# Blocks of 512 tokens, weight conversion on VectorE, and one pass over d_ff per block

## The chip, the cores and the metric

The kernel runs on one core of one Trainium2 chip. The metric is the device time of one execution in microseconds. Engines are named as the profile names them: PE (TensorE; PEld is its weight load), DVE (VectorE), ACT (ScalarE), POOL (GpSimd), SP (which issues all DMAs).

## What is computed

Three layers follow each other: linear attention with decay (retention), a feed-forward layer, and a second feed-forward layer with a softmax gate and a norm. Inputs are float32 for q, k, v; the weights are float64 in the kernel's input.

```python
# retention: B, H, S, D = 4, 8, 768, 64
gamma = 1 - 2.0 ** (-5 - arange(H))
for t in range(S):
    state = gamma * state + outer(k[t], v[t])
    y[t] = q[t] @ state / sqrt(D)
# layer 1: x is 3072 x 512, w_in 512 x 2048, w_out 2048 x 512
h = x @ w_in
g = where(h >= 1, h, where(h <= -1, 0, (h + 1) ** 2 / 4))
x2 = g @ w_out
# layer 2: w_in 512 x 1024, w_out 1024 x 512
h = x2 @ w_in
e = exp(h - max(h)); u = h * e / (sum(e) + 1e-9)
out = ((u - mean(u)) / sqrt(var(u) + 1e-6) * g_ln) @ w_out
```

## The kernel before

**Products.** Every large product is done with operands split into a high and a low part (`split`, L117: ACT copies the high part with rounding, DVE subtracts it for the low one), as high x high + low x high + high x low.

**Phase A** is layer 1, over blocks of BLK = 384 tokens (8 blocks) and 16 parts of d_ff of 128 each. A slot is one block with one part f. `moe_h` (L318) makes the first product of a slot, 12 matmuls into one PSUM bank hp, and then the activation: DVE clamps hp, ACT takes a Relu of hp and a square, DVE adds, and the split follows. `moe_out` (L346) makes the second product, 12 matmuls that add to four banks acc, two slots later (GB = 3). At a block's end the four banks are copied to xs and stored to DRAM (x2d).

**Order of the slots** (`segs`, L275): block 0 over parts 0 to 5, block 1 over parts 0 to 11, block 0 over the rest, block 1 over the rest, then blocks 2 to 7 each over all 16. Between its two stretches the sum of a block is put aside in DRAM (x2p) and added later. So new weights are taken up at about half the rate in the first 32 slots.

**Weights.** Each part f has a tile of w_in and one of w_out, 512 KB each as float64 words. `conv_w` (L133) turns one into a high and a low float32r part: ACT takes the absolute value of the high word, DVE clamps it (L140) and shifts it (L143), ACT turns the low word into a float (L142), DVE merges sign and bits (L144), POOL adds low and high words as integers (L145), ACT copies the high part (L149), and POOL, or for 14 tiles DVE, subtracts it (L150). `weights_slot` (L302) loads a tile LD = 6 or 7 slots ahead of its first use and converts it CL = 3 or 2 slots ahead. Raw tiles, converted tiles and the q, k, v of the first NF32 units share one pool of 33 tiles (tag w, L98). In the last block `w2_conv` converts the 16 tiles of layer 2, two a slot from f = 2 on.

**Attention** goes over 24 units of 128 tokens with all heads (`attention`, L157), three units to a block. The first NF32 = 6 units use float32 products, the others split operands (kh, qs). Scores get a 0/1 causal mask (DVE for the first six, a POOL selection for the others). Decay is applied to v (vdec), to the result pv (xtab, two DVE products per unit), and to the state (gdec, on POOL). The units' steps are put into slots a few slots ahead of their block (`sched`, L285).

**Phase B** is layer 2, in 24 tiles of 128 tokens: `h2` (L456), `trans` (L498), `outp` (L509).

**What sets the order.** The program is written once, in this order of slots; a planner then gives each engine its fixed list. The order of issue is the order of priority; a free engine may be given ready work of lower priority, and a tile is given out when the pool has one free. SP issues its DMAs strictly in its list's order.

Of the kernel before, what the change touches and what calls it, by code (L numbers as in the profile page):

```python
# [26 lines left out]
BLK = 384  # L27
# [6 lines left out]
# words of the high half of a float64, read as float32: 2^-127 and the largest float32r  # L34
LO_I = (0,1)
LO_O = range(4,16)
LO_2 = 0
V_POOL = 3
DMA_ORDER = -99
PSV = 0  # L40
HPW = 0
HPL = 8
SA = 6
SB = 12
LD = 6
CL = 3
HPC = 0
PHB = 3
XL_POOL = 0
QL_POOL = 0  # L50
NF32 = 6
WM_BUFS = 3
WP_BUFS = 3
QK_BUFS = 3
QS_BUFS = 1
KV_BUFS = 1
QN_BUFS = 1
GATE = 6
SM_BUFS = 3
STEP0 = 7  # L60
W0 = -4
WARM = 40
C_ACT = 0
SHIFT = 0
X2 = 22
PER = 5
HP_ATT = 1000
HP_FROM = 6
# [5 lines left out]
def kernel(  # L74
# [16 lines left out]
    order = ExitStack()  # L91
    if DMA_ORDER > -99:
        order.enter_context(tc.manual_schedule(engines={mybir.EngineType.SP}))
# [4 lines left out]
    wp = ctx.enter_context(tc.tile_pool(name="wp", bufs=33))  # L98
# [8 lines left out]
    neg1 = const.tile([128, 1], F32, tag="neg1", name="neg1")  # L107
    mask = const.tile([128, 1, C], F32, tag="mask", name="mask")
# [5 lines left out]
    def fl(t):  # L114
        return t.bitcast(F32)

    def split(src, hi, lo, hi_eng=None, lo_eng=None):  # L117
        if hi_eng is ve:
            ve.tensor_copy(hi, src)
        else:  # L120
            sc.activation(hi, src, AF.Copy)  # L121
        (lo_eng or ve).tensor_tensor(out=lo, in0=src, in1=fl(hi), op=ALU.subtract)  # L122

# [9 lines left out]
    def conv_w(raw, scale=None, lo_eng=None):  # L133
        lw, hw = raw[:, :, 0], raw[:, :, 1]
        m = cv.tile([128, 512], F32, tag="wm", name="wm", bufs=WM_BUFS)
        p = cv.tile([128, 512], F32, tag="wp", name="wp", bufs=WP_BUFS)
# [17 lines left out]
    # Heads go in pairs (even, odd); the even one takes partitions 0-63 of queries, keys and  # L154
    # state, the odd one 64-127, and TensorE works on both halves of its array at a time.
    # In x the halves of pairs 2 and 3 are swapped, and so are the rows of w_in.
    def attention(u, env):  # L157
# [6 lines left out]
        kv = (wp if exact else attp).tile([128, 2, H, D], F32, tag="w" if exact else "kv", name="kv", bufs=None if exact else KV_BUFS)  # L164
        with (ExitStack() if u < GATE else tc.issue_after(state["last_w"].ins)):
            if exact:
                qk = wp.tile([128, 2, NPAIR, C], F32, tag="w", name="qk")
                nc.sync.dma_start(qk, qk_t[b, c])
                qks = [qk, qk]
                qn = qk[:, 0]  # L170
            else:
                qks = []
                for o in range(2):
                    qk = attp.tile([128, 2, NPAIR, C], F32, tag="qk", name="qk", bufs=QK_BUFS)
                    for dup in range(2):
                        nc.sync.dma_start(qk[64 * dup:64 * dup + 64], qk_t[b, c, 64 * o:64 * o + 64])
                    qks.append(qk)
                if not first:
                    qn = attp.tile([128, NPAIR, C], F32, tag="qn", name="qn", bufs=QN_BUFS)
# [4 lines left out]
        sm = []  # L184
        if exact:
            yield
            qp = [ppool.tile([128, NPAIR, C], F32, tag=ptag, name=f"qp{o}") for o in range(2)]
            for p in range(NPAIR):
                for o in range(2):
                    r = slice(64 * o, 64 * o + 64)  # L190
                    pe.matmul(qp[o][:, p, :], qk[r, 1, p, :], qk[r, 0, p, :], start=True, stop=True)
        for o in range(2):
            if not exact:
                raw = qks[o]
                kh = cv.tile([128, NPAIR, C], F32R, tag="wm", name="kh", bufs=WM_BUFS)
                qs = attp.tile([128, NPAIR, 2, C], F32R, tag="qs", name="qs", bufs=QS_BUFS)
# [3 lines left out]
                (gp if QL_POOL else ve).tensor_tensor(out=qs[:, :, 1, :], in0=raw[:, 0], in1=fl(qs[:, :, 0, :]), op=ALU.subtract)  # L200
                yield
                t = attp.tile([128, NPAIR, C], F32, tag="sm", name="sm", bufs=SM_BUFS)
# [8 lines left out]
                gp.affine_select(out=t, in_=t, pattern=[[0, NPAIR], [1, C]], compare_op=ALU.is_ge,  # L211
                                 fill=0.0, base=0, channel_multiplier=-1)
            else:
                t = attp.tile([128, NPAIR, C], F32, tag="sm", name="sm", bufs=SM_BUFS)
# [383 lines left out]
```

## Time and profile before

| | us |
|---|---|
| median of 3 runs | 972.96 (972.27 to 973.82) |
| span of the profiled execution (first to last instruction) | 969.7 |
| its own time | not listed beside the span |
| PE busy | 936.3 (97%) |
| DVE busy | 741.9 (77%) |
| ACT busy | 455.6 (47%) |
| POOL busy | 201.0 (21%) |
| DMA | 87.03 MB, mean 90 GB/s |

Shares are means over stages with different limits, so they are to be read by stretch. A row of the profile names line, engine, operation, output and input tiles; in a group's row the mean is of one instruction's span, and spans of neighbours on one engine can overlap. Matmuls are pipelined: their mean span is longer than the time from one to the next.

### The profile page before, as it was taken

What the parts mean: (1) busy time and instruction counts of PE and PEld (TensorE: products, weight loads), DVE (VectorE), ACT (ScalarE), POOL (GpSimd) and SP (SyncE); (2) the same over time, 40 slices, a digit from 0 to 9 for tenths busy, and PEclk for the clock granted to TensorE, in tenths of its full rate; (3) what the DMA queues carried; (4) which work ended last, traced back from release to release, by engine and by line L of the source; (5) the groups of instructions that cost most, each with busy time, mean ns of one, the idle gap of its engine ahead of it and who ended that gap; (6) DMA issues with size and microseconds to landing.
All of it is one profiled execution on the core that took longest, in us unless ns stands there. A gap on an engine that the chain in (4) does not pass through costs nothing.

```text
span 969.7 us, 14961 instructions
## 1 busy us (share of the span) xinstructions
PE 936.3 (97%) x5560; PEld 856.5 (88%) x5560; DVE 741.9 (77%) x1593; ACT 455.6 (47%) x905; POOL 201.0 (21%) x177
## 2 busy tenths in 40 slices
PE   8798898999999999999999999989999999999998
PEld 7588888999999999999999999969888888888886
DVE  6999999877666666655664574997788888888885
ACT  3557676545545545544553464664433333333322
POOL 2754544212211221111220120662000000000000
PEclk9899999999999999999999999999999999999999
DMA  9902823154233232420320230311111011010000
GB/s 366 360 1 82 250 82 114 48 169 126 79 98 116 92 97 80 128 77 22 114 72 12 107 143 1 122 64 69 66 55 42 35 55 54 23 61 28 22 23 33
DMA packets 31465, 87.03 MB, mean 90 GB/s; under 512 B 4384, under 2 KB 10656, under 8 KB 31392
## 3 DMA queue, kind: packets, MB, share of 16 engines
q1 hardware_dynamic: 31392, 86.08, 26.9%
q8 instruction: 44, 0.72, 0.3%
q14 instruction: 29, 0.24, 0.1%
HBM read 71.90 MB, written 14.16 MB: 89 GB/s over the span
## 4 chain that ended last, share of the span: by engine, by line
PE 74%; DVE 18%; issue 3%; ACT 2%; DMA 2%; SPq 0%; POOL 0%; ACTq 0%; DVEq 0%; POOLq 0%
PE acc L360 19%; PE hp L325 19%; PE h2p L464 14%; PE op L516 14%; DVE wm L144 3%; DVE cs L340 3%; DVE wm L140 2%; PE pv L233 2%; PE tp L505 2%; DVE gl L122 2%; PE qp L206 2%; DVE wm L143 2%; DVE cs L337 2%; PE pv L229 2%; DVE w L150 1%
## 5 line engine op out<-in xcount | busy, mean ns | idle before, releaser
L360 PE MATMUL acc<-gh,w 128*128 128x384 f32 x1024 | 214.3, 339 | 9.6 <-ACT gh L121 7.6
L325 PE MATMUL hp<-xh,w 128*128 128x384 f32 x1024 | 209.6, 340 | 5.6 <-ACT rr L338 3.9
L360 PEld LDWEIGHTS acc<-gh,w 128*128 128x128 f32 x1024 | 180.1, 189 | 15.4 <-ACT gh L121 10.4
L325 PEld LDWEIGHTS hp<-xh,w 128*128 128x128 f32 x1024 | 179.0, 189 | 12.2 <-ACT rr L338 6.2
L338 ACT ACTIVATE rr<-hp,neg 128x384 f32<-128x384 f32 x128 | 74.1, 579 | 161.4 <-DVE cs L337 161.2
L340 DVE TENSOR_TENSOR cs<-cs,rr 128x384 f32<-128x384 f32 x128 | 86.0, 672 | 77.7 <-ACT cs L339 76.8
L360 PE MATMUL acc<-gl,w 128*128 128x384 f32 x512 | 121.7, 338 | 4.8 <-DVE gl L122 4.8
L325 PE MATMUL hp<-xl,w 128*128 128x384 f32 x512 | 111.8, 338 | 0.0
L122 DVE TENSOR_TENSOR gl<-cs,gh 128x384 fp32r<-128x384 f32 x128 | 85.5, 668 | 26.7 <-ACT gh L121 24.5
L121 ACT ACTIVATE gh<-cs 128x384 fp32r<-128x384 f32 x128 | 66.8, 522 | 65.7 <-DVE cs L340 65.5
L464 PE MATMUL h2p<-w,x2h 128*128 128x512 f32 x384 | 97.4, 395 | 0.0
L360 PEld LDWEIGHTS acc<-gl,w 128*128 128x128 f32 x512 | 90.3, 188 | 8.1 <-DVE gl L122 7.5
L337 DVE TENSOR_SCALAR cs<-hp 128x384 f32<-128x384 f32 x128 | 70.5, 551 | 32.3 <-PE hp L325 31.8
L325 PEld LDWEIGHTS hp<-xl,w 128*128 128x128 f32 x512 | 91.7, 190 | 0.5 <-DVE xl L122 0.3
L516 PE MATMUL op<-w,lh 128*128 128x512 f32 x384 | 91.4, 390 | 0.2 <-ACT lh L121 0.2
L145 POOL TENSOR_TENSOR wm<-wm,wp 128x512 int32<-128x512 int32 x48 | 69.1, 1440 | 88.0 <-DVE wm L144 70.6
L516 PEld LDWEIGHTS op<-w,lh 128*128 128x128 f32 x384 | 71.9, 188 | 15.4 <-ACT lh L121 0.5
L464 PEld LDWEIGHTS h2p<-w,x2h 128*128 128x128 f32 x384 | 70.5, 188 | 13.5
L339 ACT ACTIVATE cs<-cs,half 128x384 f32<-128x384 f32 x128 | 77.6, 606 | 2.5 <-DVE cs L337 2.5
L150 POOL TENSOR_TENSOR w<-wm,w 128x512 fp32r<-128x512 f32 x34 | 49.6, 1461 | 52.2 <-ACT w L149 51.9
L211 POOL TENSOR_SCALAR_AFFINE_SELECT sm<-sm 128x512 f32<-128x512 f32 x36 | 36.3, 1010 | 99.6 <-DVE sm L210 99.6
L254 POOL TENSOR_TENSOR state<-state,gdec 64x256 f32<-64x256 f32 x32 | 22.0, 688 | 165.1 <-DVE state L253 163.9
(79 smaller groups left out, 1299.7 us busy)
## 6 DMA issues: line engine op xcount, KB each, us to landing
qk<-in_qk_t_dram SPq DMA_DIRECT2D x72, 256.0 KB, 3.8
kv<-in_kv_t_dram SPq DMA_DIRECT2D x24, 512.0 KB, 3.8
w_raw<-in_w_in_dram SPq DMA_DIRECT2D x24, 512.0 KB, 7.3
w_raw<-in_w_out_dram SPq DMA_DIRECT2D x24, 512.0 KB, 6.7
x2d<-xs SPq DMA_DIRECT2D x32, 192.0 KB, 2.0
x2r<-x2d SPq DMA_DIRECT2D x8, 768.0 KB, 4.3
out_dram<-o SPq DMA_DIRECT2D x24, 256.0 KB, 2.0
qn<-in_qk_t_dram SPq DMA_DIRECT2D x15, 256.0 KB, 3.1
```

The costliest lines, as they stand in the source:

```text
L121: sc.activation(hi, src, AF.Copy)
L122: (lo_eng or ve).tensor_tensor(out=lo, in0=src, in1=fl(hi), op=ALU.subtract)
L145: gp.tensor_tensor(out=mi, in0=mi, in1=p.bitcast(I32), op=ALU.add)
L150: (lo_eng or gp).tensor_tensor(out=w[:, 1, :], in0=m, in1=fl(w[:, 0, :]), op=ALU.subtract)
L325: pe.matmul(hp, l[:, k * 128:(k + 1) * 128], r[:, k, :], start=(n == 0), stop=(n == 3 * KD - 1))
L337: ve.tensor_scalar(cs, hp, -1.0, 1.0, op0=ALU.max, op1=ALU.min)
L338: sc.activation(rr, hp, AF.Relu, bias=neg1)
L339: sc.activation(cs, cs, AF.Square, bias=half, scale=0.5)
L340: ve.tensor_tensor(out=cs, in0=cs, in1=rr, op=ALU.add)
L360: pe.matmul(acc[d][:, :BLK], l[:, d * 128:(d + 1) * 128], r, start=(first and m == 1), stop=(last and m == 3))
L464: pe.matmul(hps[n], l[:, k, :], w2i[k, n][part], start=(m == 0), stop=(m == 3 * KD - 1))
L516: pe.matmul(op, l[:, f, :], w2o[f][part], start=(n == 0), stop=(n == 3 * NF2 - 1))
```

## The change

Five things change together.
- BLK is 512: 6 blocks, 4 units of attention to a block, 96 slots, matmuls of 512 columns in phase A.
- Each block goes over all 16 parts at once; no sum is put aside. All 32 weight tiles have their first use in block 0's 16 slots, with loads 7 or 8 and conversions 4 or 3 slots ahead.
- `conv_w` does the integer add and the low part on DVE; a scale is folded into the last two instructions. In the last block, 2 and 1 tiles of layer 2 are converted in turn.
- The activation is max(h, square of the clamped half): the Relu and the add go, DVE takes the maximum of hp in PSUM and the square.
- Decay goes into tables: scores are multiplied by one table dmat that holds mask and decay, q is scaled by qdec (DVE in the first 8 units, POOL in the others), k by vdec on POOL, the state by ACT. xt and the POOL selections go, pv takes one bank, and 8 units instead of 6 are done in float32.

```diff
-BLK = 384
+BLK = 512
-LD = 6
-CL = 3
-NF32 = 6
-GATE = 6
+LD, CL = 7, 4
+NF32 = 2 * CPB
+GATE = 2 * CPB
...
-    def conv_w(raw, scale=None, lo_eng=None):
+    def conv_w(raw, scale=None):
...
-        gp.tensor_tensor(out=mi, in0=mi, in1=p.bitcast(I32), op=ALU.add)
-        if scale is not None:
-            ve.tensor_scalar(m, m, scale, None, op0=ALU.mult)
+        ve.tensor_tensor(out=mi, in0=mi, in1=p.bitcast(I32), op=ALU.add)
         w = wp.tile([128, 2, 512], F32R, tag="w", name="w")
-        sc.activation(w[:, 0, :], m, AF.Copy)
-        (lo_eng or gp).tensor_tensor(out=w[:, 1, :], in0=m, in1=fl(w[:, 0, :]), op=ALU.subtract)
-        return w[:, 0, :], w[:, 1, :]
+        hi, lo = w[:, 0, :], w[:, 1, :]
+        if scale is None:
+            sc.activation(hi, m, AF.Copy)
+            ve.tensor_tensor(out=lo, in0=m, in1=fl(hi), op=ALU.subtract)
+        else:
+            sc.activation(hi, m, AF.Copy, scale=scale)
+            ve.scalar_tensor_tensor(lo, m, scale, fl(hi), op0=ALU.mult, op1=ALU.subtract)
+        return hi, lo
...
-        (gp if u >= V_POOL else ve).tensor_tensor(out=kv[:, 1], in0=kv[:, 1], in1=vdec.to_broadcast([128, H, D]), op=ALU.mult)
...
+            if not first:
+                qn = attp.tile([128, NPAIR, C], F32, tag="qn", name="qn", bufs=1)
+                ve.tensor_tensor(out=qn, in0=qk[:, 0], in1=qdec, op=ALU.mult)
+        elif not first:
+            gp.tensor_tensor(out=qn, in0=qn, in1=qdec, op=ALU.mult)
+        if not last:
+            gp.tensor_tensor(out=kv[:, 0], in0=kv[:, 0], in1=vdec.to_broadcast([128, H, D]), op=ALU.mult)
...
+            if exact:
+                ve.tensor_tensor(out=t, in0=qp[o], in1=dmat[:, o], op=ALU.mult)
...
-                gp.affine_select(out=t, in_=t, pattern=[[0, NPAIR], [1, C]], compare_op=ALU.is_ge,
-                                 fill=0.0, base=0, channel_multiplier=-1)
+                ve.tensor_tensor(out=t, in0=t, in1=dmat[:, o], op=ALU.mult)
...
-        for g in range(2):
-            d = slice(2 * g, 2 * g + 2)
-            ve.tensor_tensor(out=xt[:, d], in0=pv[g], in1=xtab[:, d], op=ALU.mult)
-        split(xt, xh[:, :, tk], xl[:, :, tk], lo_eng=gp if XL_POOL else None)
+        split(pv, xh[:, :, tk], xl[:, :, tk])
...
+        if not first:
+            for p in range(NPAIR):
+                sc.activation(st[:, p, :], st[:, p, :], AF.Copy, scale=gdec[:, p, :])
...
+    def tables():
+        nc.sync.dma_start(vdec, vdec_d)
+        for o in range(2):
+            for dup in range(2):
+                nc.sync.dma_start(dmat[64 * dup:64 * dup + 64, o], xtab_d[64 * o:64 * o + 64])
+        nc.sync.dma_start(gdec, gdec_d)
+        nc.sync.dma_start(qdec, xtab_d)
+        for o in range(2):
+            ve.tensor_tensor(out=dmat[:, o], in0=dmat[:, o], in1=vdec[:, o::2].to_broadcast([128, NPAIR, C]), op=ALU.mult)
+            gp.affine_select(out=dmat[:, o], in_=dmat[:, o], pattern=[[0, NPAIR], [1, C]], compare_op=ALU.is_ge,
+                             fill=0.0, base=0, channel_multiplier=-1)
+        gp.tensor_tensor(out=qdec, in0=qdec, in1=gdec.to_broadcast([128, NPAIR, C]), op=ALU.mult)
...
-    segs = [(0, 0, SA), (1, 0, SB), (0, SA, NF), (1, SB, NF)] + [(b, 0, NF) for b in range(2, NBLK)]
+    segs = [(b, 0, NF) for b in range(NBLK)]
...
-        x = (k - 3, SA - 3 + k, X2 + 3 * k)[blk] if blk < 3 else base[blk] - NF + PER * k + SHIFT
+        x = k - CPB if blk == 0 else base[blk] - NF + PER * k + 2
...
-            at = max(first_use[f], W0 + 2 * f)
+            at = first_use[f]
...
-            ve.tensor_scalar(cs, hp, -1.0, 1.0, op0=ALU.max, op1=ALU.min)
-            sc.activation(rr, hp, AF.Relu, bias=neg1)
-            sc.activation(cs, cs, AF.Square, bias=half, scale=0.5)
-        ve.tensor_tensor(out=cs, in0=cs, in1=rr, op=ALU.add)
+        ve.tensor_scalar(cs, hp, -1.0, 1.0, op0=ALU.max, op1=ALU.min)
+        sc.activation(cs, cs, AF.Square, bias=half, scale=0.5)
+        ve.tensor_tensor(out=cs, in0=hp, in1=cs, op=ALU.max)
...
-            if f >= 2:
-                w2_conv(2)
-                w2_step(2)
+            if 2 <= f < 13:
+                w2_conv(2 - f % 2)
+                w2_step(2 - f % 2)
```

## Rows read from the trace of the kernel before

**Rows 1.** Busy time by stretch: us; PE, PEld, DVE, ACT, POOL; PEclk, DMA share, GB/s.
```profile
0.00:180.00 180.00, 157.69 (x1028) 141.84 (x1029) 167.93 (x258) 107.82 (x201) 88.53 (x73) 0.96 0.49 171
180.00:600.00 420.00, 419.50 (x2778) 407.80 (x2777) 269.53 (x494) 208.93 (x424) 73.25 (x77) 1.00 0.30 91
600.00:685.40 85.40, 78.76 (x427) 73.43 (x427) 70.04 (x100) 49.81 (x92) 39.22 (x27) 1.00 0.21 72
685.40:969.70 284.30, 280.32 (x1332) 233.46 (x1330) 234.38 (x742) 88.99 (x191) 0.00 (x0) 1.00 0.12 42
```

**Rows 2.** Chain of waits in order of time: start us, us, what.
```profile
522.08 2.08 PE hp L325 x12
...
524.16 2.08 PE acc L360 x12
...
718.38 5.48 PE h2p L464 x24
723.86 5.44 PE op L516 x24
```

**Rows 3.** Busy time by stretch, matmuls of line L325 alone.
```profile
0.00:180.00 180.00, 66.27 (x316) 0.96 0.49 171
180.00:600.00 420.00, 198.25 (x1030) 1.00 0.30 91
600.00:685.40 85.40, 36.57 (x192) 1.00 0.21 72
```

**Rows 4.** Busy time by stretch, matmuls of line L360 alone.
```profile
0.00:180.00 180.00, 59.85 (x288) 0.96 0.49 171
180.00:600.00 420.00, 200.19 (x1028) 1.00 0.30 91
600.00:685.40 85.40, 43.36 (x221) 1.00 0.21 72
```

**Rows 5.** Busy time by stretch, matmuls of line L233 (tile pv) alone.
```profile
180.00:600.00 420.00, 20.50 (x256) 1.00 0.30 91
```

**Rows 6.** Instructions of one line: min/median/max ns, first and last start us.
```profile
L140 DVE TENSOR_SCALAR wm<-wm x48: 410/420/1522, 15.4 to 657.1; 128x512 f32<-128x512 f32 x48
L143 DVE TENSOR_SCALAR wm<-wm x48: 409/417/1511, 16.1 to 659.0; 128x512 uint32<-128x512 uint32 x48
L144 DVE SCALAR_TENSOR_TENSOR wm<-w_raw,wm x48: 672/681/1776, 17.4 to 659.8; 128x512 uint32<-128x512 uint32 x48
L145 POOL TENSOR_TENSOR wm<-wm,wp x48: 1264/1404/2067, 18.3 to 660.6; 128x512 int32<-128x512 int32 x48
```

**Rows 7.** Groups of DVE, 0 to 180 us: count | busy us, mean ns | idle before.
```profile
L144 DVE SCALAR_TENSOR_TENSOR wm<-w_raw,wm 128x512 uint32<-128x512 uint32 x32 | 27.0, 846 | 0.2
L143 DVE TENSOR_SCALAR wm<-wm 128x512 uint32<-128x512 uint32 x32 | 21.9, 687 | 0.2
L140 DVE TENSOR_SCALAR wm<-wm 128x512 f32<-128x512 f32 x32 | 20.3, 640 | 0.1
L150 DVE TENSOR_TENSOR w<-wm,w 128x512 fp32r<-128x512 f32 x14 | 15.8, 1129 | 0.0
L215 DVE TENSOR_TENSOR sm<-qp,mask 128x512 f32<-128x512 f32 x12 | 8.0, 682 | 0.4 <-PE qp L191 0.4
```

**Rows 8.** Timeline of DVE, 174 to 182 us: start us, us, instruction.
```profile
175.03 0.68 DVE L144 SCALAR_TENSOR_TENSOR wm<-w_raw,wm 128x512 uint32<-128x512 uint32 x1
175.63 0.68 DVE L150 TENSOR_TENSOR w<-wm,w 128x512 fp32r<-128x512 f32 x1
...
179.72 0.69 DVE L150 TENSOR_TENSOR w<-wm,w 128x512 fp32r<-128x512 f32 x1
```

**Rows 9.** Groups of DVE over the whole span: count | busy us, mean ns.
```profile
L476 DVE TENSOR_TENSOR u<-h2p,e 128x512 f32<-128x512 f32 x48 | 32.7, 690 | 8.3 <-ACT e L474 8.2
L253 DVE TENSOR_TENSOR state<-sp,state 64x256 f32<-64x256 f32 x32 | 13.5, 421 | 6.9 <-PE sp L245 6.1
```

**Rows 10.** Waits of the DMA queue: us in total, times, longest us.
```profile
SPq L130 <- DVE wm L144: 91.3, 18, 38.1
```

More of the change, by code (lines that the diff above doesn't have):

```diff
@@ L115, in fl, with split @@
         return t.bitcast(F32)
[L117 to L122, printed above, removed]
+    def split(src, hi, lo):
+        sc.activation(hi, src, AF.Copy)
+        ve.tensor_tensor(out=lo, in0=src, in1=fl(hi), op=ALU.subtract)
     wi, wo = {}, {}
@@ L199, in attention @@
                 ve.tensor_tensor(out=kh[64:128], in0=raw[64:128, 1], in1=fl(kh[64:128]), op=ALU.subtract)
-                (gp if QL_POOL else ve).tensor_tensor(out=qs[:, :, 1, :], in0=raw[:, 0], in1=fl(qs[:, :, 0, :]), op=ALU.subtract)
+                ve.tensor_tensor(out=qs[:, :, 1, :], in0=raw[:, 0], in1=fl(qs[:, :, 0, :]), op=ALU.subtract)
                 yield
-                t = attp.tile([128, NPAIR, C], F32, tag="sm", name="sm", bufs=SM_BUFS)
                 for g in range(2):
@@ L224, in attention @@
         tk = slice(cb * C, cb * C + C)
-        pv = [ppool.tile([128, 2, C], F32, tag=ptag, name=f"pv{g}") for g in range(2)]
+        pv = ppool.tile([128, NPAIR, C], F32, tag=ptag, name="pv")
         if not first:
             for p in range(NPAIR):
-                pe.matmul(pv[p // 2][:, p % 2, :], st[:, p, :], qn[:, p, :],
-                          start=(p % 2 == 0), stop=False, skip_group_check=True)
+                pe.matmul(pv[:, p, :], st[:, p, :], qn[:, p, :],
+                          start=(p == 0), stop=False, skip_group_check=True)
@@ L231, in attention @@
         for p in range(NPAIR):
             for o in range(2):
-                pe.matmul(pv[p // 2][64 * o:64 * o + 64, p % 2, :], kv[:, 1, 2 * p + o, :], sm[o][:, p, :],
-                          start=(first and p % 2 == 0), stop=(p % 2 == 1), skip_group_check=True)
-        xt = attp.tile([128, NPAIR, C], F32, tag="xt", name="xt", bufs=1)
-        for g in range(2):
-            d = slice(2 * g, 2 * g + 2)
-            ve.tensor_tensor(out=xt[:, d], in0=pv[g], in1=xtab[:, d], op=ALU.mult)
@@ L239, in attention @@
-        split(xt, xh[:, :, tk], xl[:, :, tk], lo_eng=gp if XL_POOL else None)
+                pe.matmul(pv[64 * o:64 * o + 64, p, :], kv[:, 1, 2 * p + o, :], sm[o][:, p, :],
+                          start=(first and p == 0), stop=(p == NPAIR - 1), skip_group_check=True)
+        if not last:
+            sp = ppool.tile([128, NPAIR, D], F32, tag=ptag, name="sp")
+            for p in range(NPAIR):
+                for o in range(2):
+                    pe.matmul(sp[64 * o:64 * o + 64, p, :], kv[:, 0, 2 * p + o, :], kv[:, 1, 2 * p + o, :],
+                              start=True, stop=True)
@@ L240, in attention @@
+        split(pv, xh[:, :, tk], xl[:, :, tk])
         if last:
             return
-        sp = ppool.tile([128, NPAIR, D], F32, tag=ptag, name="sp")
-        for p in range(NPAIR):
-            for o in range(2):
-                pe.matmul(sp[64 * o:64 * o + 64, p, :], kv[:, 0, 2 * p + o, :], kv[:, 1, 2 * p + o, :],
-                          start=True, stop=True)
+        if not first:
+            for p in range(NPAIR):
+                sc.activation(st[:, p, :], st[:, p, :], AF.Copy, scale=gdec[:, p, :])
@@ L247, in attention @@
         for o in range(2):
             r = slice(64 * o, 64 * o + 64)
-            d, g = st[r, :, r], gdec[r].to_broadcast([64, NPAIR, D])
             if first:
-                ve.tensor_tensor(out=d, in0=sp[r], in1=g, op=ALU.mult)
+                ve.tensor_copy(st[r, :, r], sp[r])
             else:
-                ve.tensor_tensor(out=d, in0=sp[r], in1=d, op=ALU.add)
-                gp.tensor_tensor(out=d, in0=d, in1=g, op=ALU.mult)
+                ve.tensor_tensor(out=st[r, :, r], in0=sp[r], in1=st[r, :, r], op=ALU.add)
@@ L296, in att_slot @@
                 gens[u] = attention(u, env)
-            with (tc.high_priority(offset=HP_ATT) if HP_ATT and u >= HP_FROM else ExitStack()):
+            with (tc.high_priority(offset=HP_ATT) if u >= NF32 else ExitStack()):
                 next(gens[u], None)
@@ L363, in moe_out @@
             for d in range(KD):
-                xs = moe.tile([128, BLK], F32, tag="xs", name="xs")
+                xs = moe.tile([128, BLK], F32, tag="cs", name="xs", bufs=3)
                 a = acc[d][:, :BLK]
@@ L385 @@
         if s == min(sched):
-            for t, d in ((vdec, vdec_d), (gdec, gdec_d), (xtab, xtab_d)):
-                nc.sync.dma_start(t, d)
+            tables()
         weights_slot(s)
-        if s == DMA_ORDER:
-            order.close()
     w2 = [(w2_in[k, n], (k, n), w2i, None) for k in range(KD) for n in range(2)] + \
@@ L407 @@
         weights_slot(s)
-        if s == DMA_ORDER:
-            order.close()
         if blk == NBLK - 1:
@@ L502, in trans @@
             for n in range(2):
-                tp = (ps_a if PSV else ps_acc).tile([128, 4, 128], F32, tag="pa" if PSV else "acc", name="tp")
+                tp = ps_acc.tile([128, 4, 128], F32, tag="acc", name="tp")
                 for j in range(4):
```

94 lines of the change are left out of this document (24 added, 70 removed).

## The prediction

> **What bounds the kernel now.** I read three views in order: busy time by stretch, the chain of waits, then single instructions. The table of stretches cuts the span at 180, 600 and 685.4 us [rows 1]. Up to 180 us DVE is busy 167.93 of 180 and POOL 88.53: DVE bounds this ramp, in which 32 weight tiles are converted, and PE waits for it. From 180 to 600 PE is busy 419.5 of 420. From 600 to 685.4, the last block, DVE is busy 70 of 85.4 and PE starves a little again, because the second layer's weights are converted there. After 685.4 comes phase B, 284.3 us, PE bound.
>
> A busy PE says little of pace, so I take that from the chain [rows 2]: twelve matmuls of 384 columns in 2.08 us are 173.3 ns each, and 24 of 512 in 5.48 and 5.44 us are 227.5 ns each. The two counts of matmuls [rows 3, 4] then show what PE loses:
> - 180 to 600: 1030 + 1028 = 2058 at 0.1733 are 356.7 us. The other 63.3 us are attention; the tile pv [rows 5] has 256 matmuls here, 16 units of 16, so a unit of attention costs PE 3.96 us, its small stalls included.
> - 600 to 685.4: 192 + 221 = 413 are 71.6 us; the 14 further matmuls of the 427 in [rows 1] are phase B's, 3.2 us. So 10.6 us are lost.
> - at 180 us, when the last conversions run on DVE [rows 8], PE has done 316/12 = 26.3 slots of the first product and 288/12 = 24.0 of the second. The last conversion belongs to slot 25 of the order of issue, so PE is 1.3 slots past it with the first product and 2.3 more behind with the second.
>
> **The change, part by part.** Everything is summed to the end of phase A, 685.4 us before.
>
> *Blocks of 512.* 96 slots of 24 matmuls in place of 128: 2304 x 0.2275 = 524.2 us against 3072 x 0.1733 = 532.4. PE saves 8.2 us in all, no more: the columns are the same, only the fixed 13 ns of each matmul go. Here a rule of the Trainium skill speaks against the change: TensorE: Matmul & The Clock Gate, "Back-to-back issue gap", puts the gap at N/2.4 + 2.5 ns, an estimate of 162.5 and 215.8 ns, by which 2304 matmuls would save 2 us of 3072. The trace's 173.3 does not agree, and both sizes are measured here, so the rows decide.
>
> *Conversion on VectorE.* Before, a tile takes three DVE instructions (and a fourth for 14 tiles) plus one or two on POOL. After, it takes five on DVE: clamp, shift, the merging of words, the integer add, the low part. Undisturbed, the first two take 0.41 us and the third 0.68 [rows 6]. Their means in the ramp are 0.640, 0.687 and 0.846, that of the low part 1.129 [rows 7], and the longest reach 1.5 to 1.8 [rows 6]: an instruction that reads SBUF through both inputs, or fast, is held while POOL works. So the added work comes with less holding. For the integer add on DVE there is no row: bounds 0.41 (the fastest 512-column form) and 1.40 (POOL's median), over 32 tiles -9 to +23 us; I take 0.68, the two-input form of the same size. A tile is then 2 x 0.41 + 3 x 0.68 = 2.86 us, 32 tiles 91.5.
>
> *Maximum form.* Per slot DVE does clamp, max and low part, each near 0.69 at 512 columns, since a DVE instruction that reads a 512-column PSUM bank and SBUF takes 0.690 [rows 9]: 2.06 us a slot, against PE's 24 x 0.2275 = 5.46. ScalarE loses one of three instructions, which nobody waited for. hp is now held until the max; the bank is wanted again only three half-slots (8.2 us) later, while clamp, square and max take about 2.1, so this costs nothing outside a backlog of DVE.
>
> *Decay tables.* A unit in float32 costs DVE two products with the table (0.682 [rows 7]), one scaling of q (0.68) unless it is first, one low part (0.68) and two state updates of 0.42 [rows 9] unless it is last: eight units are 10.9 + 4.1 + 5.5 + 5.9 = 26.4 us. The tables add two products, 1.4 us, and 0.79 MB of loads in place of 0.26 ahead of the weights, 3 us at the ramp's 171 GB/s [rows 1], that lie beside attention's own work. Two units more are done in float32, which saves DVE their splitting; PE's cost per unit is taken as before. State decay moves from POOL to ScalarE, idle 72 of the first 180 us [rows 1]. In the other units the scaling of q now waits on POOL for its load, with the scaling of the keys queued behind it; PE wants both two slots (11 us) later, and POOL loses two selections a unit, so I take 0; if it came late, PE would wait at pv with all products behind it, at most 1.4 us a unit (POOL's median for a tile of this size [rows 6]).
>
> *The ramp.* Block 0 now takes up all 32 tiles in 16 slots. DVE until its last conversion (slot 12, so 13 slots by the lead above): 91.5 + 13 x 2.06 + 26.4 + 1.4 = 146.1 us of spans, 245 instructions. Neighbours overlap: two of 0.68 start 0.60 apart [rows 8]; I take 0.06 each (bounds 0 and 0.08, +14.7 and -4.9 us): -14.7. POOL keeps some ten instructions, each of which can hold one DVE instruction by 1.511 - 0.409 = 1.1 us [rows 6]: 0 to 11, I take 5. Idle time of DVE as before, 180 - 167.93 = 12.1 [rows 1]. Sum 148.5 us, against 180 before. But PE has then done only 13.3 and 11.0 of 16 slots, and 2.7 + 5.0 half-slots of 2.73 us remain, 21.0, and 2 of the last unit. The pool of 33 tiles also holds queries, keys and values of units 4 to 7 in this time. A weight load waits in SP's queue for a free tile, with the loads behind it; the longest such wait was 38.1 us [rows 10]. What that starves is unknown: 0 to 10 us, I take 3, since DVE's idle time before was small with the same waits. PE is done with block 0 at 174.5 us.
>
> *After it.* 80 slots x 5.46 = 436.8; 16 units x 3.96 = 63.4; phase B's early matmuls 3.2.
>
> *The last block.* 16 tiles over slots 2 to 12, 1.5 a slot: 1.5 x (2.86 - 0.30) + (2.06 - 0.18) = 5.7 us of DVE per slot against 5.46 of PE, so DVE falls 3 us behind over eleven slots. Two slots of look-ahead hide most of it. I take 1; bounds 0 and 10.6, the loss of before.
>
> *No partial sums.* Eight stores and eight loads go. Nothing on the bound engine waits for them beyond the few adds on DVE; 0 is taken, a gain of 2 at most.
>
> End of phase A: 174.5 + 436.8 + 63.4 + 3.2 + 1 = 678.9 us, 6.5 less than before. Phase B is the same work: 284.3 more. Span 963.2. The profiled execution's own time is not listed, only its span of 969.7; the median of the runs, 972.96, lies 3.3 above it, so I forecast 966.5.
>
> **The rivals.**
> - *The single pass starves PE (slower).* Order of issue puts conversions four slots ahead of use, and with twice as many tiles per slot PE has less to do meanwhile. If conversions wait for tiles of the pool, or their chain DVE, ScalarE, DVE leaves DVE idle, or the integer add costs nearer 1.4, block 0 ends at 190: 15.5 later, 982. It decides from an end of block 0 at 181. For it: PE has 90 us of block 0 in 174, fewer columns done at 180 than before. Against: DVE idle only 12 us in the ramp before.
> - *DVE is not held to that order (faster).* If conversions wait, DVE does slots instead, and PE is not 7.7 half-slots behind. Block 0 then ends when DVE's work ends: 148.5 + 2.7 x 1.88 + 5.5 for the last two half-slots + 2 = 161; 13.5 earlier, 953. For it: the planner fills a free engine with whatever is ready. Against: at 180 before, PE was as far behind as the order says.
> - *The gain is cancelled (no change).* DVE's work comes out 6 us longer, by an overlap of 0.035 and not 0.06: 972.5.
> - *Matmuls of 512 in phase A cost 4/3 of those of 384*, 231 ns (no fixed part): 2304 x 0.0036 = 8 us more, 975. The skill's rule above is of this kind. Against: the rows of phase B.
>
> **How the numbers follow.** This kernel's measurement can't tell less than 0.2%, 2 us, from no change. Forecast 0.41, DVE free of the order 0.16, starved 0.29, cancelled 0.12, no fixed part 0.02. Faster 0.57 (the first two), same 0.12 (the cancelled case), slower 0.31 (the other two). The range reaches to both outer cases, 953 to 982; the forecast's own is 962 to 971.
>
> **What would show it.** In the profile after: 24 matmuls of a half-run at 227 ns each; DVE's 512-column clamp near 0.41 on average in the ramp and its fourth and fifth conversion instructions near 0.68; the last conversion near 148 us and the last second-product matmul of block 0 near 174; PE busy throughout from there to the last block, with 1 us lost in that; the first product of phase B at about 679. A last conversion after 160, or much DVE idle time before it, makes the prediction wrong; so does block 0 ending before 165.

## The result, and the profile after

The changed kernel takes 933.32 us (median of 4 runs, 933.04 to 934.08), the kernel before 972.62 on the same chip (4 runs, 971.59 to 973.82): a ratio of 0.9587, 95% interval 0.9565 to 0.9609. In a second measurement, after_again, it was 934.68, ratio 0.9603 (0.9582 to 0.9625). The forecast, 966.5 with a range of 953 to 982, had the direction right and expected 6.5 us of the 39.

The profiled execution spans 931.8 us. Busy time by stretch of the changed kernel, cut where DVE's last conversion ends, where the last block begins and where phase A ends; columns as in [rows 1]:

```profile
0.00:149.00 149.00, 129.23 (x825) 99.14 (x826) 137.79 (x257) 90.14 (x159) 14.98 (x17) 0.99 0.53 191
149.00:555.00 406.00, 405.94 (x2246) 339.39 (x2245) 251.63 (x419) 170.50 (x335) 31.34 (x25) 1.00 0.30 88
555.00:646.60 91.60, 91.60 (x406) 75.88 (x405) 67.09 (x117) 45.73 (x74) 0.00 (x0) 1.00 0.22 76
646.60:931.80 285.20, 281.14 (x1335) 234.15 (x1334) 234.62 (x743) 89.39 (x191) 0.00 (x0) 1.00 0.11 41
```

Phase A ends at 646.6 in place of 685.4; phase B takes 285.2 (284.3 before), so all of the gain lies in phase A. DVE's ramp ends at 149 in place of 180, POOL does 15 us of work in it (88.5 before), and the last block, where PE starved before, has PE busy for all of its 91.6 us.

The same stretches for the matmuls of the first product (first fence, L302) and the second (second fence, L330) of the changed kernel:

```profile
0.00:149.00 149.00, 52.30 (x201) 0.99 0.53 191
149.00:555.00 406.00, 193.34 (x772) 1.00 0.30 88
555.00:646.60 91.60, 43.39 (x180) 1.00 0.22 76
```

```profile
0.00:149.00 149.00, 45.18 (x168) 0.99 0.53 191
149.00:555.00 406.00, 189.42 (x770) 1.00 0.30 88
555.00:646.60 91.60, 51.51 (x216) 1.00 0.22 76
```

When the last conversion ends, PE has done 201/12 = 16.8 slots of the first product and 168/12 = 14.0 of the second. The chain of waits gives the pace, 2.72 / 12 = 226.7 ns, in phase A as in phase B:

```profile
513.99 2.72 PE hp L302 x12
516.71 2.72 PE acc L330 x12
...
697.65 5.45 PE op L481 x24
703.98 5.49 PE h2p L429 x24
```

**Where the 39 us came from.** I split PE's time to the end of phase A in each trace by starts: from one matmul's start to the next one's. For the two products, count times pace (173.3 or 226.7 ns) is "pace"; what they take beyond it is lost, in the ramp (until 3 us after the last merging of words, L144 before and L110 after, begins; until 180 us with the order in two parts), in the middle, and in the last block. Time that begins with any other matmul (attention, the opening ones, phase B's first) is "other". Us:

```
                  end A   pace   lost: ramp  middle  last block   other
before            685.3   532.5       27.7     5.0      10.9      108.3
after             646.6   522.2       21.1     4.0       0.0       98.2
after, again      648.7   522.2       21.3     3.8       0.0      100.4
e_order           660.0   522.2       20.4     4.4       0.0      112.1
e_order2          657.7   522.2       30.5     4.1       0.0      100.0
e_order3          663.1   522.2       20.7     8.5       0.0      110.8
e_pool            674.8   522.2       28.3     7.2      10.8      105.4
e_384             695.8   532.5       35.0    21.0       0.0      106.3
e_parts           645.7   522.2       10.0     6.5       0.0      106.1
e_parts2          644.9   522.2       11.9     8.0       0.0      101.9
e_parts3          648.3   522.2       11.7    10.0       0.0      103.4
e_decay           651.6   522.2       22.3     4.9       0.0      101.2
e_relu            667.7   522.2       22.4    18.4       0.7      103.0
e_cs2             653.9   522.2       21.2     8.6       2.1       98.9
b_dve             656.7   532.5       14.3     4.7       0.1      104.1
b_max             685.7   532.5       25.8     5.1      14.7      106.5
```

Of the 38.8 us, 10.3 are the pace of wider matmuls, 6.6 the ramp, 1.0 the middle, 10.9 the last block and 10.1 the other matmuls.

The table's "lost" holds two things, PE's waits and matmuls at a lower clock. In the kernel before the granted clock is 0.50, the level of 1.2 GHz, in three stretches of the ramp; these rows lie inside them (all engines, kernel before):

```profile
23.00:29.00 6.00, 5.56 (x16) 4.28 (x16) 5.96 (x10) 2.19 (x5) 4.53 (x4) 0.50 1.03 403
47.00:50.00 3.00, 3.00 (x10) 2.45 (x10) 2.93 (x6) 1.58 (x3) 1.28 (x1) 0.50 0.02 5
91.00:94.00 3.00, 3.00 (x11) 3.00 (x10) 3.00 (x6) 1.75 (x4) 1.40 (x1) 0.51 0.14 53
```

In the kernel before 30 matmuls of the two products start in such stretches. What they take beyond their pace adds to an estimated 4.4 us (of each at most one pace more is counted, the rest being a wait). The changed kernel has no such matmul, its clock being 1.00 from 25 to 149 us, and its second profile 8 with 1.4 us; b_dve has 7 with 1.1, e_pool 33 with 6.5. So 3 to 4 of the 6.6 us of the ramp came by way of the clock.

### The profile page after: what moved, and what is told of

Its sections match the earlier page's. It is cut to its first block, busy times and chain, and to the rows that moved or that the text cites. A ratio compares the mean times of both kernels' runs of the same rounds, so it can differ in the third digit from the quotient of the medians.

```text
span 931.8 us, 12897 instructions
## 1 busy us (share of the span) xinstructions
PE 907.9 (97%) x4808; PEld 748.6 (80%) x4808; DVE 691.1 (74%) x1534; ACT 395.8 (42%) x757; POOL 46.3 (5%) x42
## 4 chain that ended last, share of the span: by engine, by line
PE 85%; DVE 9%; DMA 5%; issue 1%; ACT 0%; SPq 0%; ACTq 0%; DVEq 0%
PE acc L330 25%; PE hp L302 24%; PE h2p L429 14%; PE op L481 14%; PE tp L470 2%; DMA w_raw<-in_w_out_dram 2%; PE pv L208 2%; PE qp L186 2%; DVE wm L110 2%; DVE wm L111 1%; PE pv L204 1%; DVE w L116 1%; DMA qk<-in_qk_t_dram 1%; DMA w_raw<-in_w_in_dram 1%; DVE wm L106 1%; PE sp L214 1%
## 5 line engine op out<-in xcount | busy, mean ns | idle before, releaser
L302 PE MATMUL hp<-xh,w 128*128 128x512 f32 x768 | 199.7, 394 | 7.8 <-ACT w L115 5.4
L330 PE MATMUL acc<-gh,w 128*128 128x512 f32 x768 | 197.7, 392 | 5.6 <-ACT gh L87 5.5
L330 PEld LDWEIGHTS acc<-gh,w 128*128 128x128 f32 x768 | 142.5, 188 | 39.5 <-ACT gh L87 10.3
L302 PEld LDWEIGHTS hp<-xh,w 128*128 128x128 f32 x768 | 141.0, 188 | 40.5 <-ACT w L115 7.8
L309 ACT ACTIVATE cs<-cs,half 128x512 f32<-128x512 f32 x96 | 69.4, 723 | 135.7 <-DVE cs L308 130.6
L330 PE MATMUL acc<-gl,w 128*128 128x512 f32 x384 | 108.7, 392 | 1.1 <-DVE gl L88 1.1
L302 PE MATMUL hp<-xl,w 128*128 128x512 f32 x384 | 105.0, 390 | 0.0
L310 DVE TENSOR_TENSOR cs<-hp,cs 128x512 f32<-128x512 f32 x96 | 66.4, 691 | 42.7 <-ACT cs L309 42.5
L88 DVE TENSOR_TENSOR gl<-cs,gh 128x512 fp32r<-128x512 f32 x96 | 68.8, 716 | 33.0 <-ACT gh L87 32.3
L308 DVE TENSOR_SCALAR cs<-hp 128x512 f32<-128x512 f32 x96 | 66.1, 689 | 30.4 <-PE hp L302 29.5
L330 PEld LDWEIGHTS acc<-gl,w 128*128 128x128 f32 x384 | 71.1, 188 | 17.1 <-DVE gl L88 2.4
L302 PEld LDWEIGHTS hp<-xl,w 128*128 128x128 f32 x384 | 71.7, 188 | 15.3 <-issue 0.3
L87 ACT ACTIVATE gh<-cs 128x512 fp32r<-128x512 f32 x96 | 60.4, 629 | 55.2 <-DVE cs L310 53.8
L429 PE MATMUL h2p<-w,x2l 128*128 128x512 f32 x192 | 51.6, 390 | 0.0
```

Source lines behind the costliest of these rows:

```text
L88: ve.tensor_tensor(out=lo, in0=src, in1=fl(hi), op=ALU.subtract)
L302: pe.matmul(hp, l[:, k * 128:(k + 1) * 128], r[:, k, :], start=(n == 0), stop=(n == 3 * KD - 1))
L308: ve.tensor_scalar(cs, hp, -1.0, 1.0, op0=ALU.max, op1=ALU.min)
L309: sc.activation(cs, cs, AF.Square, bias=half, scale=0.5)
L310: ve.tensor_tensor(out=cs, in0=hp, in1=cs, op=ALU.max)
L330: pe.matmul(acc[d][:, :BLK], l[:, d * 128:(d + 1) * 128], r, start=(first and m == 1), stop=(last and m == 3))
```

## The experiments

The theory after the result (A): the conversions cost what was forecast; the failed step is PE's place when they are done, because DVE's list does slots between conversions and not conversions four slots ahead; and most of the gain is the conversion's move off POOL. B, the rival, names another part each time. Ratios are to the kernel before on the same chip.

**The order of DVE (e_order, e_order2, e_order3).** `state["last_c"]` is the low part of the conversion issued last; the clamp of a slot of block 0 is put behind it in DVE's list. e_order does so from slot 0 on, e_order2 from slot 3, e_order3 from slot 5.

```diff
-        ve.tensor_scalar(cs, hp, -1.0, 1.0, op0=ALU.max, op1=ALU.min)
+        with (tc.issue_after(state["last_c"].ins) if blk == 0 and f >= 3 else ExitStack()):
+            ve.tensor_scalar(cs, hp, -1.0, 1.0, op0=ALU.max, op1=ALU.min)
```

> The changed kernel, with one edit: in block 0 each clamp waits in DVE's list until the conversions that stand before it in the order of issue are through, four slots ahead. Theory A (the miss of the forecast is PE's place at the last conversion: DVE took conversions just in time, so PE had done 16.75 slots and not 13.3): the last conversion comes near 146 us or earlier, PE has then done about 13 slots of the first product, and the kernel takes some 17 us more than the changed kernel, about 950 us. Theory B (DVE was full either way, so the order on it costs nothing): within 2 us of the changed kernel, 931 to 935.

Measured: 947.24 us, ratio 0.9720 (0.9702 to 0.9737), 13 us over the changed kernel by ratio, where A had some 17. The last merging began 3.8 us earlier (140.0 against 143.8), and phase A still ended 13.4 later. PE stood at 13.0 and 10.7 slots at 143 us, the forecast's place. But most of the loss sits in one wait. PE's waits in e_order up to 160 us: what waited for what, us in total, times, longest:

```profile
PE pv L204 <- DVE sm L173: 14.7, 2, 13.6
PE hp L302 <- DVE cs L311: 9.6, 5, 3.4
```

That left open whether the order costs 13 us, or this one wait at 40 us (attention's masked scores, behind conversions), so two runs kept the beginning as it was.

> The changed kernel with the clamps of block 0 queued behind the conversions issued before them, but only from slot 3 on, so that the first clamps and the attention beside them stay where the changed kernel has them. The list has the 32nd conversion behind the 11th clamp (changed kernel: behind the 15th). Theory A (the order of DVE alone sets PE's place at the last conversion, and the place costs what the forecast took): last conversion some 4 us earlier, PE near 13 and 11 slots then, 943 to 949. Theory B (the first such run lost its 13 us to the one wait of 13.6 us at 40 us, where DVE converted while PE waited for masked scores at a lower granted clock; the later order costs little): 933 to 938.

> The same from slot 5 on; the list has the 32nd conversion behind the 11th clamp, the 16th behind the 5th (changed kernel: the 7th). Theory A: 940 to 949, as the run from slot 3 on, since both end in the same place. Theory B: 933 to 936, nearer to the changed kernel the later it begins.

Measured: e_order2 946.73, ratio 0.9729 (0.9704 to 0.9754); e_order3 949.59, 0.9752 (0.9731 to 0.9773). Theory A (e_order3 0.6 us past its 949); B's 933 to 938 is excluded for both. In e_order2 the matmuls of L302 (first fence) and L331, the second product (second fence), were, until 3 us after the last merging began (the first fence has a stretch of 5 us beside it):

```profile
0.00:141.00 141.00, 43.10 (x156) 0.92 0.54 199
...
70.00:75.00 5.00, 0.00 (x0) 0.50 0.31 105
```

```profile
0.00:141.00 141.00, 33.21 (x132) 0.92 0.54 199
```

These are 13.0 and 11.0 slots, and the last matmul of block 0's second products began at 174.1 us, with 174 forecast for the changed kernel (in which it began at 158.6). Where the conversions bunch, PE stands still. All engines, e_order2 and then the changed kernel:

```profile
65.00:80.00 15.00, 0.00 (x0) 0.00 (x0) 15.00 (x31) 10.76 (x19) 0.00 (x0) 0.58 0.26 94
80.00:85.00 5.00, 4.06 (x10) 3.23 (x11) 5.00 (x11) 3.11 (x6) 0.00 (x0) 0.54 0.13 39
```

```profile
65.00:80.00 15.00, 13.04 (x54) 9.56 (x53) 15.00 (x30) 10.54 (x18) 0.00 (x0) 1.00 0.32 93
80.00:85.00 5.00, 4.84 (x21) 3.68 (x20) 5.00 (x10) 3.77 (x7) 0.00 (x0) 1.00 0.09 39
```

DVE is busy all of the time in both, with 31 and 30 instructions; only which ones differs. In e_order2 PE runs no matmul from 65 to 80 us, its granted clock falls to 0.50, the level of 1.2 GHz, from 70 to 75 us in the row above, and the next five us still run at 0.54 on average. Every run with the forced order has such a wait (13.6, 16.1 and 9.2 us), and shorter ones beside it. PE's costliest waits up to 180 us in e_order2 and e_order3:

```profile
PE hp L302 <- DVE cs L311: 21.3, 5, 16.1
```

```profile
PE pv L208 <- DVE sm L173: 13.7, 3, 9.2
PE hp L302 <- DVE cs L311: 10.8, 6, 2.7
```

All of PE's waits up to 180 us add to 29.7, 31.4 and 33.6 us, against 19.7 in the changed kernel: 10 to 14 us more, where phase A ends 11 to 16 us later. From 25 to 150 us the granted clock is 0.88, 0.92 and 0.91 on average, against 1.00. So the order costs about what the forecast counted, in PE's waits for DVE and the clock's fall, and not in an evenly late PE.

**The conversion's engine (b_dve, e_pool).** b_dve is the kernel before with its conversion taken from the changed one, all else as before. e_pool is the changed kernel with the integer add, 18 of the 32 low parts and layer 2's low parts back on POOL.

```diff
-        ve.tensor_tensor(out=mi, in0=mi, in1=p.bitcast(I32), op=ALU.add)
+        gp.tensor_tensor(out=mi, in0=mi, in1=p.bitcast(I32), op=ALU.add)
...
+        (lo_eng or gp).tensor_tensor(out=lo, in0=m, in1=fl(hi), op=ALU.subtract)
...
+                wi[f] = conv_w(wraw[f][0], lo_eng=ve if f < 2 else None)
...
+                wo[f] = conv_w(wraw[f][1], lo_eng=ve if f >= 4 else None)
```

> The kernel before with the conversion on VectorE alone (integer add and low part on DVE, the scale folded in). Theory A (the move pays by itself: it ends the loss of 10.6 us in the last block and some 10 us of holding in the ramp, as the opposite edit cost 28 us on the changed kernel): about 952 us. Theory B (the move pays only with blocks of 512, since with 384 a slot gives PE too little beside DVE's work): the last block's 10 us alone, or less, 963 us or more.

> The changed kernel, with the integer add of the conversion and the low part of 18 tiles (and of layer 2's 16) back on POOL. Theory A (what POOL does holds DVE about as long as the moved instructions take on DVE): the ramp ends within 5 us of the changed kernel's, the last block loses some 9 us again, about 945 us. Theory B (work on DVE is what counts, POOL's is free): DVE has some 30 us less to do in the ramp, about 910 us.

Measured: b_dve 944.8, ratio 0.9712 (0.9691 to 0.9734). The move alone brings 28 of the 39 us: the last merging began at 164.7 (175.0 before), 13.4 us less are lost in the ramp and 10.8 less in the last block. e_pool 962.96, 0.9885 (0.9865 to 0.9906), some 29 us slower than the changed kernel: 7.2 in the ramp, 3.2 in the middle, 10.8 in the last block, 7.2 in other matmuls. Both go A's way and further than its numbers. DVE's groups in e_pool, 0 to 153 us, columns as in [rows 7]:

```profile
L110 DVE SCALAR_TENSOR_TENSOR wm<-w_raw,wm 128x512 uint32<-128x512 uint32 x32 | 31.4, 983 | 0.2
L106 DVE TENSOR_SCALAR wm<-wm 128x512 f32<-128x512 f32 x32 | 23.5, 743 | 0.1
L109 DVE TENSOR_SCALAR wm<-wm 128x512 uint32<-128x512 uint32 x32 | 23.1, 725 | 0.2
```

The changed kernel has 714, 422 and 423 ns for the same lines (rows below): with POOL in the conversion, three DVE instructions of a tile take 2.45 us in place of 1.56.

**Blocks of 384 (e_384).** The one pass kept, BLK 384 and PER 5 in place of 512 and 4.

> The changed kernel with blocks of 384 (six units in float32, units five slots apart). Theory A (a larger first block gives PE more columns to work on while the weights are converted): the fixed part of each matmul costs 8 us, and the ramp ends with fewer columns done, some 15 us more: about 956 us. Theory B (block size counts by the fixed part of a matmul alone): about 941 us.

Measured: 982.79, ratio 1.0087 (1.0070 to 1.0105). One pass with blocks of 384 is slower than the kernel before, and some 49 us slower than with 512, well past A's number. The last merging began even earlier (133.3), but a slot gives PE only 24 x 0.1733 = 4.16 us to lay beside the conversions: the ramp loses 35.0. The middle loses 21.0, part of it in waits for attention's steps; PE, 136 to 622 us:

```profile
PE qp L186 <- DVE state L227: 5.0, 6, 2.7
PE qp L186 <- DVE xl L88: 3.7, 1, 3.7
```

**The order in two parts (e_parts, e_parts2, e_parts3).** The changed kernel with the first two blocks interleaved as before, sums put aside in DRAM. In e_parts SB = 12, X2 = 22 and a step of 3; in e_parts2 as shown; in e_parts3 SB = 8, X2 = 22 and 2.5.

```diff
-    segs = [(b, 0, NF) for b in range(NBLK)]
+    SA, SB, W0, X2 = 6, 10, -4, 24
+    segs = [(0, 0, SA), (1, 0, SB), (0, SA, NF), (1, SB, NF)] + [(b, 0, NF) for b in range(2, NBLK)]
...
-        x = k - CPB if blk == 0 else base[blk] - NF + PER * k + 2
+        x = (k - CPB, SA - CPB + k, X2 + 2 * k)[blk] if blk < 3 else base[blk] - NF + PER * k + 2
...
-            at = first_use[f]
+            at = max(first_use[f], W0 + 2 * f)
```

> The changed kernel with the order of slots of the kernel before (blocks 0 and 1 in two parts each, sums put aside in DRAM), with blocks of 512. Theory A (in one pass DVE has 8 us of work per slot against 6.4 of PE; at half the rate of conversion it has 5.5, so PE loses less in the ramp): PE's 21 us of loss in the ramp go down to about 8: about 920 us. Theory B (DVE's total work decides, in whatever order; the sums put aside add some): 933 to 938 us.

> The changed kernel with blocks 0 and 1 in two parts, parts 0 to 5 and 0 to 9 first, so that block 0 ends at slot 26 and not 28, and block 2's units two slots apart. Theory A (the run before it gained 8 us in the ramp and lost them between 236 and 268 us, where the units of block 2 wait for the tiles that block 0 still holds): it is 4 to 8 us faster than the changed kernel, about 927 us. Theory B (the sums put aside cost what the ramp gains): 931 to 936 us.

> The changed kernel with the two-part order of the kernel before, block 1 over parts 0 to 7 between the stretches of block 0, sums put aside in DRAM, attention of block 2 from slot 22 on. Theory A (new weights taken up more slowly in the ramp leave PE more to do before the last conversion, with no stall left where block 2's tokens come): 926 to 930, ramp loss under 12 us instead of 21. Theory B (what the ramp gains, the units of block 2 give back): 931 to 935.

Measured: 932.25, ratio 0.9565 (0.9545 to 0.9584); 930.49, 0.9560 (2.6 us under the changed kernel by ratio, measured apart, and the two intervals overlap); 934.82, 0.9604 beside 0.9603 of the changed kernel on that chip. The ramp's loss falls from 21 to 10 to 12 us as A has it, but the middle loses 2.5 to 6 more and other matmuls take 4 to 8 more, and the time stays: A's smaller loss in the ramp, and about B's number (the first two lie 0.8 and 0.5 us under B's range). In e_parts PE waits for the second blocks of sums and tokens, 180 to 560 us:

```profile
PE hp L303 <- DVE cs L311: 2.2, 1, 2.2
PE acc L331 <- DVE xs L344: 2.1, 1, 2.1
```

So the one pass, with blocks of 512, is neutral as a whole; what the sums in DRAM cost by themselves was not told apart. No version was shown faster than the changed kernel.

**Decay tables (e_decay).** The changed kernel with the attention of the kernel before (0/1 mask, the result scaled after pv, state decay on POOL, pv in two banks), 8 units in float32.

```diff
-        pv = ppool.tile([128, NPAIR, C], F32, tag=ptag, name="pv")
+        pv = [ppool.tile([128, 2, C], F32, tag=ptag, name=f"pv{g}") for g in range(2)]
...
-        split(pv, xh[:, :, tk], xl[:, :, tk])
+        xt = attp.tile([128, NPAIR, C], F32, tag="xt", name="xt", bufs=1)
+        for g in range(2):
+            d = slice(2 * g, 2 * g + 2)
+            ve.tensor_tensor(out=xt[:, d], in0=pv[g], in1=xtab[:, d], op=ALU.mult)
+        split(xt, xh[:, :, tk], xl[:, :, tk])
```

> The changed kernel with the attention of the kernel before (0/1 mask, selection on POOL, decay on v, on the result by two products and on the state by POOL, pv in two banks), eight units still in float32. Theory A (the new form is why a unit costs PE less after the ramp, 3.5 us against 3.96): some 7 to 10 us slower than the changed kernel, about 943 us. Theory B (a unit costs less because the conversions have left POOL and the blocks are fewer, the form of decay hardly counts): 932 to 937 us.

Measured: 940.96, ratio 0.9678 (0.9653 to 0.9703), 7 to 9 us slower, near A's number; the profiled execution spans 936.8 and so shows 5 of them, spread over the ramp, the middle and the other matmuls. Part of the rest goes with the clock: two executions at a mean granted clock of 0.995 and 0.996 took 939.0 and 938.6 us, two at 0.989 and 0.990 took 942.9 and 943.5. The tables are worth a little under 1%; which of their parts is not told apart.

**The maximum form (e_relu, e_cs2, b_max).** e_relu puts the Relu and the add back into the changed kernel; the second tile's room had to come from a third buffer of cs and xs. e_cs2 takes that buffer alone. b_max is the kernel before with the maximum form alone.

```diff
-        cs = moe.tile([128, BLK], F32, tag="cs", name="cs", bufs=3)
+        cs = moe.tile([128, BLK], F32, tag="cs", name="cs", bufs=2)
+        rr = moe.tile([128, BLK], F32, tag="rr", name="rr", bufs=1)
...
+        sc.activation(rr, hp, AF.Relu, bias=neg1)
...
-        ve.tensor_tensor(out=cs, in0=hp, in1=cs, op=ALU.max)
+        ve.tensor_tensor(out=cs, in0=cs, in1=rr, op=ALU.add)
```

> The changed kernel with the activation of the kernel before (Relu on ScalarE, add on DVE; two buffers of cs). Theory A (ScalarE has room everywhere and DVE does as many instructions): within 2 us of the changed kernel, 932 to 936 us. Theory B (in the ramp ScalarE stands in the chain of every conversion, and one more instruction per slot delays that chain; the two-input add in SBUF is held by POOL where the maximum from PSUM is not): 940 us or more.

> The changed kernel with two buffers instead of three for cs and xs, the maximum form kept: control for the run with the Relu form, which lost 20 us and had to give up the third buffer for its second tile. Theory A (the third buffer was what that run missed; an activation waits for the store of an x2d copy that holds it): 946 to 955, with waits of some 10 us at the ends of blocks. Theory B (the Relu and the add cost it): 932 to 936 here.

> The kernel before with the maximum form alone. Theory A (the form takes one ScalarE instruction out of a chain nobody waits for; DVE has as many instructions as with the add): 970 to 975. Theory B (part of the 11 us that the conversion's move leaves unexplained is the form's shorter chain): 962 to 967.

> The changed kernel once more, on the chip of the next three, to carry them against each other. Both theories: 0.9587 of before, within 0.9565 to 0.9609, so 931 to 936 us.

Measured: e_relu 953.16, ratio 0.9791 (0.9775 to 0.9808); e_cs2 943.05, 0.9695 (0.9665 to 0.9725); b_max 971.3, 0.9987 (0.9976 to 0.9998); the changed kernel beside the last two 934.68. e_relu's 20 us are thus in halves the missing buffer (9 us) and the Relu form on top of it (9 us, by ratios of two chips). For e_relu B's "940 us or more" holds, but not B's place for it: the ramp loses 1.3 us more, the middle 14.4. e_cs2 lies between its two theories. In the kernel before the form is worth 1 us. DVE's clamp waits for a store that holds its tile, in the changed kernel, e_cs2 and e_relu, over the span:

```profile
DVE cs L308 <- DMA x2d<-xs: 0.2, 1, 0.2
```

```profile
DVE cs L308 <- DMA x2d<-xs: 2.8, 3, 1.4
```

```profile
DVE cs L311 <- DMA x2d<-xs: 7.9, 5, 2.5
```

So one half of what the form gives here is room: without the second tile there is a third buffer, and a block's last copies don't stop the next block's first slots. Of the other half the runs show only that it, too, is lost in the middle (18.4 us in e_relu, 8.6 in e_cs2); its cause stays open.

**The parts don't add.** Taken out of the changed kernel one at a time, the conversion's move costs 29 us, the blocks of 512 49, the maximum form with its buffer 18 to 20, the tables 7 to 9: far more than 39 together. Put into the kernel before alone, the move gains 28 and the maximum form 1.

## Why the forecast missed

**Right, but in part by luck: the end of DVE's conversions.** Last conversion forecast for 148.5, measured 148.26 (start of the last L116). DVE's groups in the changed kernel, 0 to 149 us:

```profile
L110 DVE SCALAR_TENSOR_TENSOR wm<-w_raw,wm 128x512 uint32<-128x512 uint32 x32 | 22.8, 714 | 0.0
L111 DVE CUSTOM_DVE_ANT_0 wm<-wm,wp 128x1024 uint16<-128x1024 uint16 x32 | 22.1, 695 | 0.1
L116 DVE TENSOR_TENSOR w<-wm,w 128x512 fp32r<-128x512 f32 x32 | 21.9, 688 | 0.0
L109 DVE TENSOR_SCALAR wm<-wm 128x512 uint32<-128x512 uint32 x32 | 13.5, 423 | 0.1
L106 DVE TENSOR_SCALAR wm<-wm 128x512 f32<-128x512 f32 x32 | 13.3, 422 | 0.1
L308 DVE TENSOR_SCALAR cs<-hp 128x512 f32<-128x512 f32 x16 | 11.0, 687 | 0.1
```

A tile is 2.94 us where 2.86 was taken; the integer add, which had no row, is 0.695 where 0.68 was taken from the two-input form; the holding is all but gone, min/median/max in ns:

```profile
L106 DVE TENSOR_SCALAR wm<-wm x48: 411/424/448, 21.9 to 601.3; 128x512 f32<-128x512 f32 x48
```

The longest is 448 where [rows 6] have 1522, and e_pool has 1508 for the same line. The Trainium skill, SBUF — State Buffer, "SBUF: two separate sides", calls the port pair of DVE and GpSimd an exclusive lock held for a whole instruction; the trace agrees, and gives the price, up to 1.1 us. In the changed kernel's first 149 us four of DVE's 257 instructions take more than 0.7 us (0.94, 1.15, 1.28, 1.53); each of them begins while an instruction of POOL runs and ends 0.54 to 0.55 us after it.

The sum met its time although single terms did not. DVE's spans add to 157.0 us and not 146.1: the tiles are 94 in place of 91.5, and 16 clamps, 15 maxima and 15 low parts take 31.6 where 13 slots were to take 26.8. Against that, spans overlap by 157.0 - 137.8 = 19.2 us where 14.7 was taken, there is little holding where 5 was taken, and DVE was idle 149 - 137.79 = 11.2 us, with 12.1 taken from before.

**Failed: PE's place at that time.** The step was "But PE has then done only 13.3 and 11.0 of 16 slots, and 2.7 + 5.0 half-slots of 2.73 us remain". Measured 369 matmuls of the products (201 + 168), forecast 24.3 x 12 = 292: 77 x 0.2267 = 17.5 us. The last matmul of block 0's second products began at 158.6 where 174 was forecast; an end of block 0 before 165 was one of the prediction's own signs of being wrong. The lead of 1.3 and 2.3 slots came from one point of before, where the order of issue says slot 25 and 24 clamps had run. DVE's groups of the kernel before, up to the start of its last merging (the 32nd L144):

```profile
L144 DVE SCALAR_TENSOR_TENSOR wm<-w_raw,wm 128x512 uint32<-128x512 uint32 x31 | 26.3, 851 | 0.2
...
L337 DVE TENSOR_SCALAR cs<-hp 128x384 f32<-128x384 f32 x24 | 13.1, 546 | 0.0
```

The same group of clamps in the changed kernel, up to the start of its last merging:

```profile
L308 DVE TENSOR_SCALAR cs<-hp 128x512 f32<-128x512 f32 x15 | 10.3, 688 | 0.1
```

There the order of issue says slot 12, and 15 clamps had run: the planner takes slots as they become ready, and conversions between them. Before took up one f in two slots, after one in each; I read before's agreement as an outcome of that, not as a rule. The other runs bear this out: where the order in two parts says slot 23 to 25 for the last conversion, 20 to 26 clamps had run (b_dve 26, e_parts 22), and where the one pass says 12, 14 or 15 had, whatever the conversion cost (e_pool 14), unless the order was forced (11 or 12). The forecast weighed this as a rival, "DVE is not held to that order", at 0.16; it was what happened, with block 0's end near the 161 us that this rival gave, and the forced orders show what the rejected reading costs. The rival's total of 953 was still 20 us too long, by the terms that follow.

**The rest after 149 us.** The forecast had 530.4 from there to the end of phase A, measured 497.6. Besides the 17.5: a unit of attention costs (406 - 1542 x 0.22667) / 16 = 3.53 us and not 3.96, 6.9 for the 16 units that this row of their tile pv (L208) counts:

```profile
149.00:555.00 406.00, 18.62 (x256) 1.00 0.30 88
```

the allowance of 3 for waits of the weights' pool and the 2 for a unit's rest were not needed (SP's longest such wait was 42.7 us, 38.1 in [rows 10], but up to 150 us neither PE nor DVE shows a wait for a weight load):

```profile
SPq L96 <- DVE wm L110: 110.7, 17, 42.7
```

the pace is 226.7 and not 227.5 (1.6), the last block lost 0 and not 1, phase B's early matmuls took 2.3 and not 3.2. Sum 32.9; with phase B's 0.9 more, 0.5 more up to 149, and 1.5 us outside the span in place of 3.3, these are the 33 us of the miss. Why the units are cheaper is not settled. After the ramp, the 256 matmuls of pv that take the scores of the same 16 units last, from start to start and waits included, 74 ns each before, 72 in b_dve and 68 in b_max, but 60 in the changed kernel, 64 in e_decay (old attention) and 62 in e_pool; e_384, with the new attention, has 67 (18 units). That points to the block's width and not to the form of attention; why a wider block would do it, no run shows.

**Right: the smaller steps.** Blocks of 512 gave 10.3 us of pace, 8.2 forecast. For the 768 matmuls fewer that is 13.3 ns each; the prediction named 13 ns, but its 8.2 us, with phase B's 227.5, are 10.7 each. 4/3 of 173.3 ns, the rival without a fixed part, is out. By the Trainium skill's formula that the forecast set aside (TensorE: Matmul & The Clock Gate, "Back-to-back issue gap") a matmul of 512 would be an estimated 215.8 ns; the section gives it for a single matmul's gap, and the trace's runs of twelve, with 226.7, do not agree with it. The order in one pass, partial sums and all: neutral. Phase B: +0.9. The last block: 1 us left of 10.6 was taken, 0 measured. **Not seen ahead:** that the maximum form and the tables, priced at about 0, are worth 18 to 20 and 7 to 9 us inside the changed kernel; and that the conversion's move is worth 28 us in the old order too: the sum was made for the whole change only, and there its gain stood against a place of PE that did not come.

**The rivals.** "The single pass starves PE" was wrong for 512 but describes e_384. "The gain is cancelled" is out: DVE's last conversion did not come later than summed.

## What to carry to other kernels

A lead between engines read off at one time of one kernel is the outcome of that kernel's order and rates: before carrying it over, count what the bound engine's list has done by then, here clamps against conversions, at several times. Where two engines hold each other, price the move of work by the fastest instance of each instruction on both sides, and look for every stage that runs it: here the last block gave 10.9 us and the ramp 6.6. Make the sum for each part of a compound change alone as well; the part that carries it then stands out.

## What was not expected of the hardware

An int32 add of two 128x512 tiles on DVE appears as a custom operation on 128x1024 uint16 and takes 0.695 us, half of POOL's 1.40 [rows 6]. A PE that stood still for 16 us cost more than that wait: the clock was still at 0.54 in the five us after it (e_order2, 80 to 85). Waits count here beyond their length: the kernel before ran 30 matmuls of its ramp's products at 0.50, the changed one none, or 8 in its second profile.
